# Two weight blocks loaded behind the first keys and queries of an attention and mixture-of-experts kernel

## The chip, the cores and the metric

The kernel runs on one core of one Trainium2 chip. The metric is device time in microseconds (us) of one execution; three timed runs of the kernel before gave 814.26, 817.00 and 824.21 us, median 817.0 us. The core's engines are TensorE (PE, with its weight load PEld), VectorE (DVE), ScalarE (ACT) and GpSimd (POOL); SyncE (SP) issues nearly all of the DMAs. Each engine works through its own list of instructions strictly in order, and semaphores join the lists.

## The reference

Three layers follow one another; all is float32, and the weights of the second layer arrive as 64-bit floats.

```python
# 1. attention, 2 x 8 heads, 576 rows, head size 64; only the 32 largest scores of a row count
scores = scale * np.matmul(q, k.transpose(0, 1, 3, 2))
kth = np.partition(scores, -32, axis=-1)[..., -32:-31]
scores = np.where(scores >= kth, scores, -1e9)
attn = softmax(scores)                      # spelled out in the reference
x = np.matmul(attn, v)                      # to 1152 tokens x 512
# 2. dense layer: w_in 512 x 2048, w_out 2048 x 512
h = x @ w_in
g = np.maximum(h, 0.0) + alpha * np.minimum(h, 0.0)
x = g @ w_out
# 3. eight experts, 512 -> 1024 -> 512; each token goes to its two best, by noisy gate logits
h = np.maximum(x[mask] @ w1[e], 0.0)
out[mask] += top2_w[mask, k, None] * (h @ w2[e])
```

## The kernel before, in words

**Order of the work.** The kernel is straight-line code whose order comes from a small planner (class Order, line 150 on). Every piece of work is a Python generator that asks for engines, buffers and results; the planner keeps a rank for each and a modelled time, and gives a free engine to the waiting step of the lowest rank. A step of the form (engine, cost, extra, shift) may carry a shift that is added to its rank for that one step. What the planner decides is frozen as the order of instructions on each engine; on the chip an engine waits where the planner's time was too early.

**Attention.** For each batch and each pair of heads the keys are loaded (kb, load_pair), split in a rounded part and its remainder (prep: ACT copy L450, then a subtraction L461 on POOL or, for the first pair, on DVE) and transposed on PE (L423) into kp. Queries (qb) go the same way (L510, L514, L423, then a copy to qt on ACT, L428, or on DVE, L430). A unit is two heads of one tile of 128 queries. PE forms the scores (L582), ACT copies them (L598), DVE folds the two halves (L612, L616, L619) and finds the 32nd largest by rounds of MAX8 and MATCH_REPLACE8 (L633, L636); ACT and POOL build the masked exponentials (L670, L672, L676); PE transposes them (L693) and multiplies by the values (vb, L717).

**Dense layer.** Its 16 blocks of w_in and w_out give 32 conversions, `convert(i)`, i even for w_in and odd for w_out. One loads 128 x 512 words of 64 bits (raw, 512 KB, L820 or L822), makes 32-bit floats of them with three DVE instructions (L835, L837, L840), tests their size on ACT (magnitude, L890 and L894), splits them in a rounded part (ACT, L874) and a remainder (POOL, L876) and stores both (L856). The blocks are multiplied (L948, L992) for five groups of token tiles; the first group uses them as they are converted.

**Fillers.** Where the planner's model has PE idle early on, it inserts matmuls of ones (L1728) whose result nobody reads.

**Experts.** After the last group come gate, routing, gathers and the expert layers (L1507, L1542).

The lines around the change: XD is a new constant beside the others (line 73 of the changed kernel, so that all later lines stand one number higher there); the load step of convert; the rank with which the main part adds convert. There, t is the time planned for the first group, CB is 20.0 and CT is 7.5, so conversion 0 has rank 1.5 before and conversion 1 has rank 9.0. The keys of the second pair have rank 0.3, the values 0.8 and up, the split of the second pair of keys 5.0, the first unit's top-k 8.0.

Of the kernel before, what the change touches and what calls it, by code (L numbers as in the profile page):

```python
# [53 lines left out]
NR, NF, NR2, CB, KE, CT = 3, 2, 2, 20.0, 0, 7.5  # L54
# [15 lines left out]
DG, DX, DS = 1.0, 2.0, 0.5  # L70
YC, YL = 0.65, 4.0
NK, FB1 = 4, 12.0
OL, PL = 8.0, 10.0
BEGIN = (("DMA", 1.7), ("ACT", 1.9), ("DVE", 1.5), ("POOL", 1.0))


def split(v):
    return v.bitcast(F32)
# [31 lines left out]
PE, ACT, DVE, POOL, DMA = "PE", "ACT", "DVE", "POOL", "DMA"  # L110
# [25 lines left out]
class Order:  # L136
# [99 lines left out]
    def take(self, *names, room=1):  # L236
        def got():
            for w in names:
                if self.held.get(w, 0) < room:
                    self.held[w] = self.held.get(w, 0) + 1  # L240
                    return w
        return "until", got

    def give(self, what):
        self.held[what] -= 1
        self.given[what] = self.now
        self.at(self.now, 1, self.scan)

    def mark(self, *what):
        self.made.add(what)  # L250
        self.at(self.now, 1, self.scan)

    def need(self, *what):
        return "until", lambda: what in self.made
# [9 lines left out]
def block_kernel(ctx: ExitStack, tc: tile.TileContext, q, k, v, w_in, w_out, alpha,  # L264
# [19 lines left out]
    order = Order()  # L284
# [525 lines left out]
    def convert(i):  # L810
        fb, half = divmod(i, 2)
        w = w_out if half else w_in
        u = 2 if WIDE else 1
        yield take("raw", room=NR)
        yield DMA, 0.75 * u, 2.0
        raw = a1.tile([128, 512 * u], I32 if WIDE else F32, name="raw", bufs=NR)
        if WIDE:
            w = w.bitcast(I32)
        if half:
            nc.sync.dma_start(raw, w[fb * 128:(fb + 1) * 128, :])  # L820
        else:
            nc.sync.dma_start(raw.rearrange("p (c f) -> p c f", c=4),  # L822
                              w[:, fb * 128 * u:(fb + 1) * 128 * u].rearrange("(c p) f -> p c f", p=128))
        if WIDE:
            if i:
                yield need("wf", i - 1)
            yield take("wf", room=NF)
            mark("wf", i)
            f = a2.tile([128, 512], I32, name="wf", bufs=NF)
            rv = raw.rearrange("p (n t) -> p n t", t=2)  # L830
            hi, lo = rv[:, :, 1], rv[:, :, 0]
            yield take("words")
            yield DVE, 0.6
            t = ps.tile([128, 512], F32, name="y1").bitcast(I32)
            V.tensor_scalar(t, hi, 3, 0x3FFFFFFF, op0=OP.logical_shift_left, op1=OP.bitwise_and)  # L835
            yield DVE, 0.65
            V.scalar_tensor_tensor(t, hi, -0x40000000, t, op0=OP.bitwise_and, op1=OP.bitwise_or)  # L837
            order.add(order.rank + 20, magnitude(i, hi.bitcast(F32)))
            yield DVE, 0.65
            V.scalar_tensor_tensor(f, lo, 29, t, op0=OP.logical_shift_right, op1=OP.bitwise_or)  # L840
            f = f.bitcast(F32)
            yield FIN
            give("words")
        else:
            f = raw
        wt, tag = yield from halves(fb, half, f, POOL, fb >= KE)
        yield FIN
        order.add(order.rank, keep(wsc[fb, half], split(wt).rearrange("p a n -> p (a n)"), "hl", fb, half))
        give("wf" if WIDE else "raw")
        if fb < KE:  # L850
            yield need("hl", fb, half)
            give(tag)

    def keep(dst, src, *key):
        yield DMA, 1.5, KL
        nc.sync.dma_start(dst, src)  # L856
        yield FIN
        mark(*key)
# [5 lines left out]
    def halves(fb, half, f, eng, use=True):  # L864

        if use and fb:
            yield need("wt0", half, 0, fb - 1)
        tag = yield take(*places[half])
        wt = a2.tile([128, 2, 512], R32, name=tag)
        if use:  # L870
            WT[0, fb, half] = wt, tag
            mark("wt0", half, 0, fb)
        yield ACT, 0.52
        nc.scalar.activation(wt[:, 0], f, AF.Copy)  # L874
        yield (POOL, pool(512)) if eng == POOL else (DVE, dve(512))
        (nc.gpsimd if eng == POOL else V).tensor_sub(wt[:, 1], f, split(wt)[:, 0])  # L876
        if use:
            order.add(order.rank, marked("wt", 0, fb, half), order.now + (pool(512) if eng == POOL else dve(512)) + HOP)
        return wt, tag
# [6 lines left out]
    def magnitude(i, hi):  # L886
        yield take("mag")
        yield ACT, act(512)
        mag = a1.tile([128, 512], BF, name="mag")
        nc.scalar.activation(mag, hi, AF.Square)  # L890
        yield FIN
        give("raw")
        yield ACT, act(512, 2)
        nc.scalar.activation(mag, mag, AF.Relu, bias=bcon[:, 3:4], scale=-2.0 ** 28, accum_out=least[:, i:i + 1])  # L894
        yield FIN
        give("mag")
        mark("mag", i)
# [6 lines left out]
    def load_kept(g, i, half):  # L904
        fb = block_of(g, i)
        yield need("hl", fb, half)
        if g or i:
            yield need("wt0", half, *((g, 0 if g and i == KB else i - 1) if i else (g - 1, 15)))
        tag = yield take(*places[half])
        yield DMA, 1.5, 2.0  # L910
        wt = a2.tile([128, 2, 512], R32, name=tag)
        nc.sync.dma_start(split(wt).rearrange("p a n -> p (a n)"), wsc[fb, half])
        WT[g, i, half] = wt, tag
        mark("wt0", half, g, i)
        yield FIN
        mark("wt", g, i, half)
# [868 lines left out]
    t = 0.0  # L1785
    for g, ts in enumerate(GROUPS):
        t = max(t, ready[g])
        late = g == len(GROUPS) - 1
        work = len(ts) * 1.3
        step = work if late else max(work, (ready[g + 1] - t) / 16)  # L1790
        for fb in range(16):
            for half in range(2):
                if (g and fb >= KB) or (not g and fb < KE):
                    order.add(t - 10.0 + 4 * half + MO, load_kept(g, fb, half), max(t - 40.0, 0.0))
                if not g:
                    order.add(min(t - CB + 4 * half, 1.5 + CT * (2 * fb + half)), convert(2 * fb + half))
            order.add(t + MO, moe1_block(g, fb))
            t += step
        ranks["gate", g] = t - (GB if late else 0.0)
        order.add(ranks["gate", g], gate(g))  # L1800
# [258 lines left out]
```

## Time and profile before

| what | value |
|---|---|
| timed runs | 814.26, 817.00, 824.21 us; median 817.0 us |
| profiled execution, its own time | 811.02 us |
| its span, first to last instruction | 809.3 us |
| busy: PE, PEld, DVE, ACT, POOL | 752.3, 685.8, 606.2, 506.4, 358.1 us |
| mean granted TensorE clock | 0.972 of 2.4 GHz |
| moved by DMA | 156.62 MB, mean 194 GB/s |

The profile shows one execution. Busy time is a sum over stages with different limits, so a stage has to be read by itself: a table of busy time in stretches tells which engine has no idle time left there, the timeline of one engine shows the gap before each instruction and what ended it, and the order of issue of the loads is in the rows of SP. The profiled execution was 6.0 us shorter than the median of the timed runs.

### The profile page before, as it was taken

The numbers are of one execution on the slowest core, as the hardware profiler recorded it, in microseconds if no ns is written. First come the engines' busy times: TensorE is split into PE (matmuls) and PEld (weight loads), VectorE is DVE, ScalarE is ACT, GpSimd is POOL, SyncE is SP. The second block draws the span as 40 slices with busy tenths as digits, with TensorE's granted clock in tenths as the row PEclk, the third lists the DMA queues.
The fourth block names the chain that finished last, engine by engine and source line by source line (L and its number), as shares of the span: only waits on it lengthen the run. The fifth ranks groups of instructions, "written<-read, shape, count | busy, mean of one in ns | idle before, by whom it ended". The sixth has DMA issues, their size and how long they took to land. (4 is left out here: it accounts for less than half of the span.)

```text
span 809.3 us, 15510 instructions
## 1 busy us (share of the span) xinstructions
PE 752.3 (93%) x5238; PEld 685.8 (85%) x5238; DVE 606.2 (75%) x1713; ACT 506.4 (63%) x1081; POOL 358.1 (44%) x402
## 2 busy tenths in 40 slices
PE   8999878769999999999999999989899998999994
PEld 6888767668898998899988988878799997999983
DVE  6999999998988888898889545167567756667632
ACT  6878897897588778576747642264545544455331
POOL 3655665665575555454445434302422424131313
PEclk9999998688999999999999999999999999999998
DMA  9444689851446402465247559988889988986631
GB/s 277 138 157 122 196 284 321 291 177 64 134 148 193 156 28 94 150 229 181 104 132 234 183 181 304 347 218 198 239 247 242 264 212 245 254 255 180 203 103 59
DMA packets 99851, 156.62 MB, mean 194 GB/s; under 512 B 15902, under 2 KB 65582, under 8 KB 99764
## 3 DMA queue, kind: packets, MB, share of 16 engines
q1 hardware_dynamic: 94260, 145.04, 58.6%
q0 software_dynamic: 5504, 10.51, 4.5%
q8 instruction: 43, 0.70, 0.4%
q14 instruction: 44, 0.36, 0.1%
HBM read 126.76 MB, written 29.34 MB: 193 GB/s over the span
## 5 line engine op out<-in xcount | busy, mean ns | idle before, releaser
L672 POOL TENSOR_TENSOR low<-s_sb,low 128x576 f32<-128x576 f32 x72 | 102.5, 1425 | 81.6 <-ACT low L670 81.6
L948 PE MATMUL h_ps<-xh,wi 128*128 128x256 f32 (+1 forms) x576 | 123.9, 294 | 3.3 <-DVE gf L966 2.6
L948 PEld LDWEIGHTS h_ps<-xh,wi 128*128 128x128 f32 x576 | 98.0, 196 | 8.4 <-DVE gf L966 4.4
L633 DVE MAX8 tk<-rest 128x8 f32<-128x296 f32 x216 | 97.7, 459 | 1.1
L992 PE MATMUL y<-wo,gh 128*128 128x512 f32 x288 | 96.7, 417 | 1.3 <-ACT gh L976 1.3
L979 POOL TENSOR_TENSOR gl<-gf,gh 128x256 fp32r<-128x256 f32 (+1 forms) x80 | 56.6, 709 | 67.3 <-ACT gh L976 65.5
L948 PE MATMUL h_ps<-xl,wi 128*128 128x256 f32 (+1 forms) x288 | 83.4, 289 | 0.0
L717 PE MATMUL x_ps<-vb,pT 128*128 128x64 f32 (+1 forms) x640 | 79.7, 270 | 3.7 <-ACT pT L696 3.3
L717 PEld LDWEIGHTS x_ps<-vb,pT 128*128 128x128 f32 (+1 forms) x640 | 74.7, 187 | 9.9 <-ACT pT L696 6.6
L1298 ACT ACTIVATE w2o<-raw 128x512 fp32r<-128x512 f32 (+1 forms) x60 | 40.4, 711 | 57.2 <-PE x_ps L1542 31.6
L1301 DVE TENSOR_TENSOR w2o<-raw,w2o 128x512 fp32r<-128x512 f32 (+1 forms) x60 | 45.5, 790 | 35.6 <-ACT w2o L1298 28.8
L1507 PE MATMUL s_ps<-xeh,w2i 128*128 128x336 f32 (+1 forms) x256 | 64.9, 315 | 3.8 <-DVE hl L1523 3.8
L1542 PE MATMUL y<-hh,w2o 128*128 128x336 f32 (+1 forms) x288 | 66.9, 316 | 0.0
L636 DVE MATCH_REPLACE8 rest<-tk,rest 128x296 f32<-128x296 f32 x144 | 64.8, 451 | 0.0
L1507 PE MATMUL h_ps<-xeh,w2i 128*128 128x336 f32 (+1 forms) x256 | 63.3, 313 | 0.4 <-DVE hl L1523 0.4
L676 ACT ACTIVATE low<-low,bias 128x576 f32<-128x576 f32 x72 | 55.7, 774 | 12.3 <-POOL low L672 12.2
L582 PE MATMUL s_ps<-kp,qt 128*128 128x288 f32 (+2 forms) x336 | 60.9, 310 | 1.9 <-DVE rest L616 1.9
L598 ACT ACTIVATE s_sb<-s_ps 128x576 f32<-128x576 f32 x72 | 46.9, 651 | 22.9 <-PE s_ps L582 22.3
L992 PE MATMUL y<-wo,gl 128*128 128x512 f32 x144 | 58.6, 407 | 2.1 <-POOL gl L979 1.4
L670 ACT ACTIVATE low<-s_sb,bias 128x576 f32<-128x576 f32 x72 | 55.6, 774 | 7.7 <-POOL bias L641 7.6
L1323 POOL DMA_INDIRECT xg<-x,meta x21 | 25.7, 1225 | 72.2 <-DMA xl<-xg 28.9
L948 PEld LDWEIGHTS h_ps<-xl,wi 128*128 128x128 f32 x288 | 56.5, 196 | 0.7 <-issue 0.3
(315 smaller groups left out, 2069.4 us busy)
## 6 DMA issues: line engine op xcount, KB each, us to landing
raw<-in_moe_w_dram SPq DMA_DIRECT2D x60, 512.0 KB
wi<-wsc SPq DMA_DIRECT2D x48, 512.0 KB
wo<-wsc SPq DMA_DIRECT2D x48, 512.0 KB
raw<-in_moe_w_in_dram SPq DMA_DIRECT2D x16, 512.0 KB
raw<-in_moe_w_out_dram SPq DMA_DIRECT2D x16, 512.0 KB
wsc<-wi SPq DMA_DIRECT2D x16, 512.0 KB
wsc<-wo SPq DMA_DIRECT2D x16, 512.0 KB
raw<-in_moe_w_dram SPq DMA_DIRECT2D x48, 128.0 KB
```

The costliest lines, as they stand in the source:

```text
L582: nc.tensor.matmul(s_ps[:, j, o:o + c1 - c0], l, r[:, c0:c1], start=(i == 0), stop=(i == len(steps) - 1 and (c < 4 or c1 != S)))
L633: V.max(tk[:, 8 * i:8 * i + 8], src)
L636: V.match_replace(rest, tk[:, 8 * i:8 * i + 8], src, -3.0e38)
L670: nc.scalar.activation(low, SC[ht], AF.Relu, bias=bi[:, 1:2], scale=-BIG)
L672: nc.gpsimd.tensor_sub(low, SC[ht], low)
L676: nc.scalar.activation(low, low, AF.Exp, bias=bi[:, 0:1], scale=SCALE, accum_out=SM[part][:, col:col + 1])
L717: nc.tensor.matmul(o, pT[:, i, cs], vb[b, hh // 2][:, s, i * 64:(i + 1) * 64], start=(first and hh == h and i == 0), stop=False)
L948: nc.tensor.matmul(h_ps, l[:, d, :], r[:, d, 0:gn], start=(n == 0), stop=(n == 11))
L979: nc.gpsimd.tensor_sub(gl, gf, split(gh))
L992: nc.tensor.matmul(Y1[g][t], l[:, t * 128:(t + 1) * 128], r, start=(i == 0 and n == 0), stop=(i == 15 and n == 2))
L1507: nc.tensor.matmul(h_ps, l[:, d, s * 128:(s + 1) * 128], r[:, d, :], start=(n == 0), stop=(n == 11))
L1542: nc.tensor.matmul(YP[e][b][:, 0:c], l[:, s, bs], r[:, 0:c], start=(fb == 0 and n == 0), stop=(fb == 7 and n == 2))
```

## The change

Conversions 0 and 1 (the first blocks of w_in and w_out) both get rank 3.0, where they had 1.5 and 9.0. Their load step carries a shift of -2.65, so the loads stand at rank 0.35, right behind the keys of the second pair (0.3). Nothing is computed in another way and no work is added or taken out, but for what the planner decides differently in consequence.

```diff
+XD = -2.65
...
         yield take("raw", room=NR)
-        yield DMA, 0.75 * u, 2.0
+        yield DMA, 0.75 * u, 2.0, XD if i < 2 else 0.0
...
                 if not g:
-                    order.add(min(t - CB + 4 * half, 1.5 + CT * (2 * fb + half)), convert(2 * fb + half))
+                    order.add(3.0 if 2 * fb + half < 2 else min(t - CB + 4 * half, 1.5 + CT * (2 * fb + half)), convert(2 * fb + half))
```

The queue of SP, from the second pair of keys on, in the kernel before (kb keys, vb values, vtail and qtail the last 64 rows of values and queries, raw the 64-bit weights):

```order
L374 DMA kb<-in_k_dram 128x2x256
L374 DMA vb<-in_v_dram 128x2x256
L396 DMA vtail<-in_v_dram 64x4x64 x2
L383 DMA qtail<-in_q_dram 64x8x64
L374 DMA vb<-in_v_dram 128x2x256 x2
L374 DMA kb<-in_k_dram 128x2x256
L374 DMA vb<-in_v_dram 128x2x256
L822 DMA raw<-in_moe_w_in_dram 128x4x256
L820 DMA raw<-in_moe_w_out_dram 128x1024
L374 DMA kb<-in_k_dram 128x2x256
```

The same place in the changed kernel:

```order
L375 DMA kb<-in_k_dram 128x2x256
L823 DMA raw<-in_moe_w_in_dram 128x4x256
L821 DMA raw<-in_moe_w_out_dram 128x1024
L375 DMA vb<-in_v_dram 128x2x256
L375 DMA kb<-in_k_dram 128x2x256
L397 DMA vtail<-in_v_dram 64x4x64 x2
L384 DMA qtail<-in_q_dram 64x8x64
L375 DMA vb<-in_v_dram 128x2x256 x3
L375 DMA kb<-in_k_dram 128x2x256
```

The two weight blocks have moved ahead of all values and of the third pair of keys, which itself has moved ahead of three of the values.

The list of DVE from the second remainder of queries on, before (s_sb and s_ps are the scores, tk and rest the folded ones, wf the converted weights):

```order
L514 TENSOR_TENSOR low<-qb,low 128x512
L430 CAST qt<-y_211 128x512
L612 TENSOR_TENSOR tk<-s_sb,s_ps 128x288
L616 TENSOR_TENSOR rest<-s_sb,s_ps 128x288
L619 MAX tk<-rest 128x8
L633 MAX tk<-tk 128x8
L636 MATCH_REPLACE rest<-tk 128x296
L633 MAX tk<-rest 128x8
L612 TENSOR_TENSOR tk<-s_sb,s_ps 128x288
L835 TENSOR_SCALAR y_287<-raw 128x512
L616 TENSOR_TENSOR rest<-s_sb,s_ps 128x288
L837 SCALAR_TENSOR_TENSOR y_287<-raw,y_287 128x512
```

The same place in the changed kernel:

```order
L515 TENSOR_TENSOR low<-qb,low 128x512
L836 TENSOR_SCALAR y_206<-raw 128x512
L838 SCALAR_TENSOR_TENSOR y_206<-raw,y_206 128x512
L613 TENSOR_TENSOR tk<-s_sb,s_ps 128x288
L841 SCALAR_TENSOR_TENSOR wf<-raw,y_206 128x512
L617 TENSOR_TENSOR rest<-s_sb,s_ps 128x288
L836 TENSOR_SCALAR y_260<-raw 128x512
L620 MAX tk<-rest 128x8
L838 SCALAR_TENSOR_TENSOR y_260<-raw,y_260 128x512
L634 MAX tk<-tk 128x8
L841 SCALAR_TENSOR_TENSOR wf<-raw,y_260 128x512
L613 TENSOR_TENSOR tk<-s_sb,s_ps 128x288
```

Conversion 0 now stands ahead of the first fold and conversion 1 is woven into the first one and the second; the copy of the last quarter of queries (L430) has left DVE's list, and ACT's list has one more copy to qt in its place. From the third conversion on, the conversions stand at the same count of folds as before (within one, for one of them). On POOL the remainders of both conversions (L876) now stand ahead of the splits of the third and the fourth pair of keys (L461). PE's list has 407 fillers in place of 424; behind its last score matmul there are 59 in place of 47, 22 in place of 15 in one run of them.

## Rows read from the trace of the kernel before

**Rows 1.** The page, part 2: busy tenths in 40 slices of 20.2 us.
```profile
PE   8999878769999999999999999989899998999994
DVE  6999999998988888898889545167567756667632
```

**Rows 2.** Stretches of 20 us: length, busy (count) by engine, clock, DMA share, GB/s.
```profile
100.00:120.00 20.00, 13.96 (x95) 12.05 (x96) 19.27 (x49) 19.94 (x48) 14.54 (x16) 0.97 0.85 279
...
140.00:160.00 20.00, 14.61 (x74) 13.03 (x73) 18.99 (x50) 16.61 (x39) 12.27 (x14) 0.66 0.84 285
160.00:180.00 20.00, 13.29 (x90) 11.52 (x88) 19.19 (x52) 17.81 (x43) 14.61 (x16) 0.91 0.60 208
180.00:200.00 20.00, 19.65 (x130) 18.47 (x131) 17.01 (x57) 14.66 (x34) 11.18 (x14) 0.83 0.11 41
...
220.00:240.00 20.00, 20.00 (x151) 18.59 (x150) 17.46 (x59) 17.41 (x43) 14.68 (x19) 1.00 0.52 172
```

**Rows 3.** Stretches of 10 us, same columns.
```profile
10.00:20.00 10.00, 8.83 (x71) 6.97 (x69) 8.75 (x22) 7.64 (x19) 4.66 (x6) 1.00 0.97 315
20.00:30.00 10.00, 9.23 (x78) 7.75 (x77) 9.84 (x29) 10.00 (x23) 7.44 (x9) 1.00 0.48 173
```

**Rows 4.** Timeline of DVE: start, length, instruction, idle before and what ended it.
```profile
8.65 0.68 DVE L514 TENSOR_TENSOR low<-qb,low 128x512 fp32r<-128x512 f32 x1
...
10.16 0.69 DVE L430 CAST qt<-y 128x512 fp32r<-128x512 f32 x1 [0.83 <-PE y L423]
...
10.77 0.44 DVE L612 TENSOR_TENSOR tk<-s_sb,s_ps 128x288 f32<-128x288 f32 x1
...
14.18 0.46 DVE L612 TENSOR_TENSOR tk<-s_sb,s_ps 128x288 f32<-128x288 f32 x1 [0.54 <-ACT s_sb L598]
...
15.05 0.69 DVE L835 TENSOR_SCALAR y<-raw 128x512 int32<-128x512 int32 x1 [0.42 <-DMA raw<-in_moe_w_in_dram]
...
16.99 0.67 DVE L840 SCALAR_TENSOR_TENSOR wf<-raw,y 128x512 int32<-128x512 int32 x1
```

**Rows 5.** Timeline of SP's queue, same columns: issues of loads.
```profile
3.22 0.51 SPq L374 DMA_DIRECT2D kb<-in_k_dram  x1
3.77 0.47 SPq L374 DMA_DIRECT2D vb<-in_v_dram  x1
...
7.68 0.37 SPq L374 DMA_DIRECT2D kb<-in_k_dram  x1
...
9.46 0.37 SPq L822 DMA_DIRECT2D raw<-in_moe_w_in_dram  x1
```

**Rows 6.** DMA view, 0 to 20 us: rate in 40 slices of 0.5 us.
```profile
GB/s 0 0 0 43 106 342 266 360 378 306 209 317 356 346 354 354 309 250 225 198 287 348 350 346 348 350 348 348 402 401 389 346 359 348 348 217 0 123 246 401
```

**Rows 7.** Timeline of ACT, POOL and PE, columns of rows 4: first users of the loads.
```profile
3.60 0.63 ACT L450 ACTIVATE prep<-kb 128x512 fp32r<-128x512 f32 x1 [1.57 <-DMA kb<-in_k_dram]
...
5.74 0.63 ACT L510 ACTIVATE low<-qb 128x512 fp32r<-128x512 f32 x1 [1.51 <-DMA qb<-in_q_dram]
...
12.81 0.63 ACT L450 ACTIVATE prep<-kb 128x512 fp32r<-128x512 f32 x1 [0.52 <-DMA kb<-in_k_dram]
...
13.52 1.27 POOL L461 TENSOR_TENSOR prep<-kb,prep 128x512 fp32r<-128x512 f32 x1 [2.42 <-ACT prep L450]
...
16.67 0.79 PE L582 MATMUL s_ps<-kp,qt 128*128 128x288 f32 x4
```

**Rows 8.** Lines L428, L835 (shortest/median/longest ns); DVE's waits, 20 to 200 us.
```profile
L428 ACT ACTIVATE qt<-pt x16: 575/600/624, 9.2 to 360.4; 128x512 fp32r<-128x512 f32 x16
...
L835 DVE TENSOR_SCALAR y<-raw x32: 666/678/695, 15.1 to 175.3; 128x512 int32<-128x512 int32 x32
...
DVE tk L612 <- ACT s_sb L598: 4.5, 6, 2.2
```

**Rows 9.** Timeline of PE behind the last attention unit, columns of rows 4.
```profile
497.76 1.81 PE L1728 MATMUL x_ps<-ones 128*128 128x256 bf16 x15
...
500.38 0.50 PE L992 MATMUL y<-wo,gl 128*128 128x512 f32 x1 [0.34 <-issue]
```

## The prediction

> **What bounds the kernel now.** I first read where each engine has no time left. The slices of the page [rows 1] show the two regimes: VectorE (DVE) is at nine tenths from the second slice to about 180 us, and from there to the end of the dense layer TensorE (PE) is. The table of stretches [rows 2] makes this sharper: from 100 to 180 us DVE is busy for 19.0 to 19.3 of 20 us while PE stands idle for 5 to 7 us in the three stretches shown, because it waits for attention units; from 180 us PE is busy for 19.65 and later for 20.00 of 20 us. So up to 180 us the kernel goes as fast as DVE's list, and after that PE works off what is left. A microsecond by which DVE's list runs earlier before 180 us lets PE begin its full stretch a microsecond earlier, and should come out at the end; work merely moved within full DVE time gains nothing.
>
> The change touches the first 20 us. There DVE is not yet full: 8.75 of 10 us from 10 to 20, against 9.84 from 20 to 30 [rows 3]. The timeline tells why [rows 4]: behind the second remainder of queries, which ends at 8.65 + 0.68 = 9.33 us, DVE stands 0.83 us for a transposition (before the copy L430), 0.54 us for the second pair of scores and 0.42 us for the first weight block: 1.79 us in all. After that DVE meets no gap in that view up to 20 us. The conversions are 32 times three instructions of some 0.68 us [rows 8], a stock of work that needs nothing but its weights; idle time early on can be filled with it, if the weights are there.
>
> **The change, part by part.**
>
> *When the first block arrives.* The queue of SP and the bytes decide it. Before, the block was issued at 9.46 us [rows 5] and DVE, which waited for it, got it at 15.05 [rows 4], 5.6 us later, because the loads ahead of it had to move first. I test whether loads arrive in the order of issue by adding up bytes along the rate view [rows 6], sizes from the tile shapes (4 bytes per number, 0.262 MB for a pair of keys or values, 0.524 MB for half the queries or a weight block, 0.131 MB for the rows at the end). First keys: 0.262 MB have passed at 3.1 us, used at 3.60. First queries: 0.786 MB at 4.65, used at 5.74. Third pair of keys: 3.015 MB at 11.97, used at 12.81, where ACT waited for it [rows 7]. First weight block: 3.80 MB at 14.20, used at 15.05. Both late ones came 0.85 us behind their bytes, so order of issue explains them. In the changed queue the first weight block is the sixth load: 0.262 + 0.524 + 0.131 + 0.524 + 0.262 + 0.524 = 2.23 MB, which pass at 9.37; plus 0.85 gives an estimate of **10.2 us**. It takes the place of the first values, issued at 3.77 [rows 5], so the issue itself is early enough. The second block follows at 2.75 MB, 11.2 + 0.85 = 12.1 us.
>
> *What DVE gains.* Its list now has the conversion right behind 9.33. It waits to 10.2, 0.87 us, about what it waited before for the transposition. From there it has a conversion whenever a fold is not ready: three instructions of conversion 0 with the first fold between them, then conversion 1, whose block (12.1) is needed only about 13 us. So the later gaps of 0.54 and 0.42 are filled, and idle time falls from 1.79 to 0.87: **-0.92 us**. The copy L430, 0.69 us on DVE [rows 4], goes to ACT: **-0.69**. Sum **-1.6 us**.
>
> *What it costs elsewhere.* ACT takes one copy more, 0.60 us [rows 8], and the early part of two conversions; from 10 to 20 us it has 10.00 - 7.64 = 2.4 us free, which hides them, but from 20 to 30 it has none [rows 3]. Without that cover the copy would cost 0.6. The third pair of keys comes later by bytes: 3.28 MB, 12.73 + 0.85 = 13.6 in place of 12.81; and on POOL a remainder of 1.27 us (as the split of the same size [rows 7]) now precedes its split. That split began at 13.52. Conversion 0 ends on DVE about 12.7 (10.2, two instructions, the first fold, one more), ACT rounds it by 13.4, POOL is through with its remainder at 14.7, and then splits the keys to 16.0. PE has the third score matmul, which began at 16.67 [rows 7], behind their transpositions in its list; it goes to some 17.3, ends about 18.1, and its copy on ACT is through by some 18.8, and DVE comes to the third fold only about 19.5 (start to start its listed instructions take 0.37 to 0.6 us from 10.2 on). That is hidden, with 0.7 us to spare. The values come up to 3 us later; the first multiplication by them needs a finished top-k and its exponentials, so nothing waits. The fourth pair of keys has the same bytes ahead of it and does not move. Unmoved also is the rest of the conversions, which stand at the same folds as before.
>
> *SP.* Before, the issues at 7.68 and 9.46 stood behind earlier waits [rows 5]; the moved blocks, sixth and seventh in the queue, follow the second keys at 3.22 directly. No engine waits for SP in the rows of this stretch.
>
> *Fillers.* Behind the last score matmul there are 12 more, 7 of them in the run that had 15. That run took 1.81 us, 0.12 us each [rows 9]; if PE has other work there, 12 of them cost up to 1.4 us. I take zero, since after the run PE still stood 0.34 us before the third matmul of the block [rows 9]: what it was to multiply was not there. The bound of 1.4 goes into the range.
>
> The bounds of the sum: at best all 1.79 and the 0.69 are gained, -2.5 us. Against the profiled execution's own 811.0 us the forecast of -1.6 gives 809.4; that execution was 6.0 us under the median of the timed runs, so on their footing it is 817.0 - 1.6 = **815.4 us**.
>
> **The rivals.**
>
> *ACT takes it back (0.22).* ACT is full from 20 to 30 us, and again from 100 to 120 with 19.94 of 20 [rows 2, 3]. If it sets the pace there, a DVE that is 1.6 us ahead waits for the copies of the scores; it waits for them 4.5 us in six waits between 20 and 200 us as it is [rows 8]. Then the lead is spent and the time is that of before, **817.0**. Against it: 4.5 of 180 us is little, and DVE's 19.0 to 19.3 of 20 show it as the tighter one.
>
> *The blocks come late, and the first fold stands behind them: slower (0.13).* DVE works strictly in order, so fold one, ready at 10.77, cannot pass conversion 0. If the loads in flight share the engines and do not go in order, the first block lands with the second, the first values and the third keys, at 3.28 MB, 13.6 us. DVE then waits 13.6 - 9.33 = 4.3 us, against a stock of 1.79 + 0.69 = 2.5: **+1.8 us, 818.8**. It decides from a landing at 9.33 + 2.5 = 11.8 us on. For it speaks that the changed queue puts half a megabyte more behind it at once; against it the two loads that came in order within 0.85 us. The Trainium skill, "DMA: Bandwidth & Descriptors", section "Queues, rings and completion order", says that completion is not first-in, first-out per issuing engine, since a later load may finish its writes before an earlier one. By that rule the stall could come, and the sum would be the 818.8 of this rival; the trace, where the two loads that can be checked came in order of issue, does not show it here.
>
> *PE's clock falls elsewhere (0.15).* From 140 to 200 us the granted clock is 0.66, 0.91 and 0.83 between its two levels of 1.2 and 2.4 GHz, after stretches in which PE stood idle [rows 2]. From 180 on PE is the bound, and 20 us at 0.83 cost it 20 x 0.17 = 3.4 us. The order of PE's list shifts all along, so this stretch may come out at full clock, **815.4 - 3.4 = 812.0**, or be followed by another one like it, **818.8**; I take both alike.
>
> *The change does nothing it says (0.05).* The rank may move the loads but DVE's lead may be lost in its own few waits before 180 us, without ACT: 817 again. The forecast itself has 0.45.
>
> **How the numbers follow.** The time is that of the forecast, 815.4 us. The range is set by the runs more than by the cases: the cases lie between 812.0 and 818.8, the bound of the gain under the profiled execution's own time gives 811.0 - 2.5 = 808.5, and at the top I add some 2 us for the scatter of a median, whose runs before lay between 814.3 and 824.2. That gives 808 to 821 us. About 2% (16 us) is what a measurement of this kernel can tell from no change. No case comes near it: 0.02 for faster by more (800.7 or less), 0.02 for slower by more (833.3 or more), left for something unforeseen, and 0.96 within.
>
> **What would show it right or wrong.** In the profile of the changed kernel, the first conversion on DVE should begin at 10.0 to 10.5 us, with a wait for the weight load before it; a start behind 11.8 would be the slower rival. DVE should then show no gap to 20 us and be busy for over 9.5 of the 10 us from 10 to 20. The third pair of keys should reach ACT at about 13.6, the third fold should begin near 19.5 without a wait. The lead should still stand at 180 us: conversion 31, whose first instruction began at 175.3 us before [rows 8], should begin some 1.6 us earlier, in spite of ACT's full stretches; if it begins at 175, ACT took the lead back. Lastly the first instant at which PE is full should come earlier by the same. A change of more than 5 us in either direction would be wrong by more than this sum can hold, and would have to lie in PE's clock or in the run of fillers behind 480 us.

## The result, and the profile after

The changed kernel takes 822.48 us (median of 21 runs, 815.27 to 832.93), the kernel before in the same job 815.52 (median of 21): 7.0 us more, a ratio of medians of 1.0085. The ratio taken over the faster runs of each kernel, as all ratios below are, is **1.0104, with a 95% interval of 1.0064 to 1.0144**, some 8.5 us. So the kernel is slower by 7.0 to 8.5 us, which is within the 2% called the same. The forecast was 815.4 us, 1.6 less than before, with a range of 808 to 821. The profiled execution took 824.87 us, its span 823.1 at a mean clock of 0.962; before it was 811.02, 809.3 and 0.972. The two profiles lie 13.8 us apart, so they show more than the typical loss.

I read the profile in the order of time. The timeline of DVE after, with the columns of [rows 4], shows the front of the list as it was forecast:

```profile
8.88 0.69 DVE L431 CAST qt<-h_ps 128x512 fp32r<-128x512 f32 x1 [1.26 <-PE h_ps L424]
...
9.68 0.68 DVE L515 TENSOR_TENSOR low<-qb,low 128x512 fp32r<-128x512 f32 x1
10.28 0.69 DVE L836 TENSOR_SCALAR y<-raw 128x512 int32<-128x512 int32 x1
...
11.88 0.46 DVE L613 TENSOR_TENSOR tk<-s_sb,s_ps 128x288 f32<-128x288 f32 x1 [0.18 <-ACT s_sb L599]
...
13.21 0.69 DVE L836 TENSOR_SCALAR y<-raw 128x512 int32<-128x512 int32 x1
...
20.14 0.45 DVE L613 TENSOR_TENSOR tk<-s_sb,s_ps 128x288 f32<-128x288 f32 x1 [0.29 <-ACT s_sb L599]
```

The first conversion starts at 10.28 and waits for nothing, so its block was there. The gaps of [rows 4] behind the second remainder of queries (L515 now) are gone but for 0.18 us, and the next is 0.29 at the third fold. A new one of 1.26 us stands ahead of the remainder, which ends at 10.36 in place of 9.33 in this execution; other executions of this front differ there, as the account of the prediction shows. SP issued both blocks right behind the second keys (3.23), where [rows 5] has the values:

```profile
3.77 0.47 SPq L823 DMA_DIRECT2D raw<-in_moe_w_in_dram  x1
4.29 0.50 SPq L821 DMA_DIRECT2D raw<-in_moe_w_out_dram  x1
```

The stretches of after, columns of [rows 2] (the two of 10 us answer to [rows 3]):

```profile
10.00:20.00 10.00, 9.22 (x75) 7.46 (x74) 9.63 (x25) 9.29 (x21) 6.17 (x6) 1.00 1.11 342
20.00:30.00 10.00, 9.24 (x77) 7.62 (x75) 9.39 (x27) 9.34 (x21) 6.23 (x8) 1.00 0.35 122
100.00:120.00 20.00, 14.40 (x78) 12.83 (x78) 19.17 (x52) 19.84 (x47) 13.57 (x16) 0.74 0.84 277
140.00:160.00 20.00, 13.41 (x76) 11.92 (x75) 18.50 (x49) 18.05 (x42) 13.36 (x14) 0.76 0.87 304
160.00:180.00 20.00, 17.30 (x94) 15.93 (x95) 19.70 (x55) 17.70 (x43) 12.91 (x15) 0.67 0.52 166
180.00:200.00 20.00, 19.06 (x135) 17.30 (x135) 16.64 (x58) 14.81 (x33) 9.94 (x14) 0.90 0.18 66
```

DVE has 9.63 of 10 us where it had 8.75. PE's granted clock lies elsewhere than before (0.74 against 0.97 from 100 to 120 us, 0.67 against 0.91 from 160 to 180). Conversion 31 starts 2.8 us earlier than in [rows 8]:

```profile
L836 DVE TENSOR_SCALAR y<-raw x32: 666/680/705, 10.3 to 172.5; 128x512 int32<-128x512 int32 x32
```

So nothing is lost in the part that was changed. Where it is lost, a few instants of both timelines tell (us; the last score matmul L582, the last x of the attention L782, the last matmuls by w_in and w_out, L948 and L992, the scatter of the routing slots, the end of the span; lines of before):

| | last scores | last x | last w_in | last w_out | slots | span |
|---|---|---|---|---|---|---|
| before | 446.4 | 468.1 | 522.3 | 529.5 | 554.6 | 809.3 |
| after | 444.9 | 469.1 | 526.9 | 538.8 | 565.9 | 823.1 |

After is 1.5 us ahead at the last scores and 9.3 behind at the last matmul by w_out: 10.8 us in between, where the diff touches nothing. Another 2.0 us are lost up to the slots and 2.5 in the expert layers behind them. The waits of PE in that part (engine, tile, line, releaser: us in total, times, longest), first before, 444 to 532 us:

```profile
PE y L992 <- ACT gh L976: 1.2, 1, 1.2
PE y L992 <- POOL gl L979: 0.8, 1, 0.8
PE h_ps L948 <- ACT gf L960: 0.5, 1, 0.5
PE y L992 <- issue: 0.3, 1, 0.3
```

and after, 443 to 541 us:

```profile
PE h_ps L1729 <- ACT gf L961: 2.9, 1, 2.9
PE y L993 <- DMA wo<-wsc: 1.5, 1, 1.5
PE y L993 <- ACT gh L977: 1.5, 2, 0.9
PE y L993 <- issue: 1.0, 1, 1.0
PE y L993 <- POOL gl L980: 0.8, 1, 0.8
PE x_ps L718 <- ACT pT L697: 0.7, 1, 0.7
PE s_ps L949 <- DMA wi<-wsc: 0.7, 1, 0.7
```

2.8 us of waits have become over 9, and dense weights and a copy of ACT are among them. ACT's timelines say why. Before, ACT rounded the third block of expert weights (L1298) early, with a wait of 1.09 us:

```profile
490.63 1.06 ACT L1298 ACTIVATE w2i<-raw 128x1024 fp32r<-128x1024 f32 x1 [1.09 <-DMA raw<-in_moe_w_dram]
```

After:

```profile
518.68 0.42 ACT L977 ACTIVATE gh<-gf 128x256 fp32r<-128x256 f32 x1 [0.94 <-PE y L993]
528.63 1.06 ACT L1299 ACTIVATE w2i<-raw 128x1024 fp32r<-128x1024 f32 x1 [9.53 <-DMA raw<-in_moe_w_dram]
529.59 0.36 ACT L961 ACTIVATE gf<-h_ps 128x256 f32<-128x256 f32 x1
```

L1299 is the same rounding. It now waits 9.53 us for its load, and the last copies of the dense layer (gf, L961) stand behind it in ACT's list. The first of them starts at 529.59, although PE had its products by w_in ready at about 524.8: 4.8 us late. (The Trainium skill, "Perfetto Trace Analysis", section "Tensor Engine Instruction (MATMUL, LD_WEIGHTS)", calls ACT's execution queue strict first-in, first-out; these 4.8 us are what that costs here.) The load is the third of the expert weights. SP's timeline after:

```profile
514.61 3.08 SPq L1283 DMA_DIRECT2D raw<-in_moe_w_dram  x4
517.79 1.46 SPq L913 DMA_DIRECT2D wo<-wsc  x2
```

and before:

```profile
481.67 1.85 SPq L1282 DMA_DIRECT2D raw<-in_moe_w_dram  x4
```

Before, it went out 33 us earlier; now it goes out ahead of the last two blocks of w_out, which come late in their turn. The fillers of [rows 9] are now 22, and PE stands 1.00 us behind them:

```profile
498.19 2.58 PE L1729 MATMUL x_ps<-ones 128*128 128x256 bf16 x22
...
502.24 0.50 PE L993 MATMUL y<-wo,gl 128*128 128x512 f32 x1 [1.00 <-issue]
```

Of the 10.8 us, idle time of PE is 6.5 (9.5 against 3.0, summed over stretches). The other 4.3 are busy time: 12 more fillers at 0.12 us, about 1.2 us of a lower clock behind 527 us, and 1.1 us for eight matmuls by the values (48 in place of 40) that before stood ahead of the last scores; some 0.6 us are not accounted for.

### The profile page after: what moved, and what is told of

Same layout as the page of the kernel before. It is cut to its first block, busy times and chain, and to the rows that moved or that the text cites. A ratio compares the mean times of both kernels' runs of the same rounds, so it can differ in the third digit from the quotient of the medians.

```text
span 823.1 us, 15442 instructions
## 1 busy us (share of the span) xinstructions
PE 756.5 (92%) x5221; PEld 688.8 (84%) x5221; DVE 605.8 (74%) x1712; ACT 510.0 (62%) x1082; POOL 354.2 (43%) x402
## 5 line engine op out<-in xcount | busy, mean ns | idle before, releaser
L1299 ACT ACTIVATE w2o<-raw 128x512 fp32r<-128x512 f32 (+1 forms) x60 | 40.4, 711 | 58.5 <-PE x_ps L1543 33.0
L1302 DVE TENSOR_TENSOR w2i<-raw,w2i 128x1024 fp32r<-128x1024 f32 x36 | 43.9, 1220 | 23.8 <-ACT w2i L1299 21.6
L993 PEld LDWEIGHTS y<-wo,gh 128*128 128x128 f32 x288 | 50.0, 195 | 9.7 <-issue 2.0
```

The costliest lines, as they stand in the source:

```text
L993: nc.tensor.matmul(Y1[g][t], l[:, t * 128:(t + 1) * 128], r, start=(i == 0 and n == 0), stop=(i == 15 and n == 2))
L1302: V.tensor_sub(lo, x, split(hi))
```

## The experiments

**Theories.** T1: the planner, whose modelled times the change has shifted, writes another order behind the attention, and that order is the loss; its most visible piece is the third expert load. T2: the loss is the run of fillers behind 480 us. T3: the moved work costs the time itself, through PE's clock between 100 and 220 us.

The planner makes a tool of itself here: adding to the *planned* cost of one conversion step, which no instruction carries, changes the order from that step on. So each front can be joined to either order behind it.

**The changed front with the order of before behind it.** To the changed kernel:

```diff
-            yield DVE, 0.6
+            yield DVE, 0.6 + (2.0 if i == 28 else 0.0)
```

> The changed kernel, with 2 us more of planned time for the first step of conversion 28: the changed kernel's order for the first 100 issues of SP and 406 rows of DVE (to about 160 us, first conversion at 10.3 us), then the kernel before's for the last 508 issues of SP, 1531 rows of DVE and 764 of ACT. It is the mirror of the run with the old front and the new rest. T1 (the front is as good as forecast, the loss lies in the order behind it): ratio 0.994 to 1.000, conversion 31 near 173 us, the last output-weight matmul near 527 us, so the forecast of 1.6 us gained holds for this kernel. Rival T3 (the front gives its lead back through PE's clock between 100 and 200 us whatever follows): ratio 1.001 to 1.006.

Measured: **0.9995 [0.9958, 1.0032]**. Conversions from 10.5 to 172.1 us, last scores 444.5, last w_out 528.4, 83.9 us apart as before. The loss is gone with the front left in. In its profile DVE runs 1.9 us ahead of before on the same instructions from 425 to 510 us, and 0.2 behind by 536. The forecast gain of 1.6 us (0.998) lies within the interval, as does none.

**The front of before with the changed order behind it.** To the kernel before, the same line with 1.5 at i == 28:

> The kernel before, with 1.5 us more of planned time for the first step of conversion 28. The order is the kernel before's for the first 109 issues of SP and 407 rows of DVE (to about 160 us, first conversion on DVE at 15.1 us), and the changed kernel's for the last 501 issues of SP, 1531 rows of DVE and 763 of ACT. T1: the loss appears without the changed front, ratio 1.007 to 1.013, ACT waits near 9 us for the third load of expert weights. T3: nothing is lost, ratio 0.997 to 1.003.

Measured: **1.0116 [1.0078, 1.0153]**. The whole loss without any of the change. Last scores to last w_out take 95.5 us, and ACT's timeline has the wait:

```profile
533.41 1.06 ACT L1298 ACTIVATE w2i<-raw 128x1024 fp32r<-128x1024 f32 x1 [10.13 <-DMA raw<-in_moe_w_dram]
```

Compared instruction by instruction, these two kernels go over from the one order to the other between 159 and 190 us. They settle it between T1 and T3. Two more joints, with 2.0 at i == 20 and at i == 6 in the changed kernel:

> The changed kernel, with 2 us more of planned time (not of real time) for the first step of conversion 20. The order is the changed kernel's for the first 82 issues of SP and 321 rows of DVE (to about 100 us), and the kernel before's for the last 528 issues of SP, 1599 rows of DVE and 825 of ACT, the stretch behind the attention among them. Theory T1 (the order that the planner writes behind the attention costs the time): the loss goes, ratio to the kernel before 0.996 to 1.001, the last output-weight matmul near 529 us and the last ACT row of the second weights without its 9.5 us wait. Rival T3 (the work moved to the first 20 us itself costs it, through the clock that PE is granted behind it): the loss stays, ratio 1.006 to 1.012, with PE's clock under 0.8 in two stretches of 20 us between 100 and 200 us.

> The changed kernel, with 2 us more of planned time for the first step of conversion 6: the changed front for the first 60 issues of SP and 196 rows of DVE, and then the kernel before's order for the last 561 issues of SP and 1821 rows of DVE, so that only the first 60 us or so differ from the kernel before. T1: ratio 0.996 to 1.001. T3: ratio 1.001 to 1.006, with PE's clock under 0.8 in the stretch 100 to 120 us, where the kernel before has 0.97.

Measured: 1.004 [1.0002, 1.0079] and 1.0003 [0.9976, 1.0029]. In the first, DVE is 0.7 us ahead of before on the same instructions at 130 us and 1.9 behind at 159, with PE's clock at 0.81 from 120 to 140, where before had 0.85, and 0.77 against 0.97 from 100 to 120; in the second the clock from 100 to 120 is 0.99. The first lies outside what T1 said (0.996 to 1.001), the second within. As the front stands in both, and in the run of 0.9995, and the intervals overlap, the 0.4% of the first need not be the front's; what it is stays open. If T3 holds anything, it is a few tenths of a per cent.

**The halves of the change.** Loads alone, and rank alone, each on the kernel before:

```diff
-        yield DMA, 0.75 * u, 2.0
+        yield DMA, 0.75 * u, 2.0, (-1.15, -8.65)[i] if i < 2 else 0.0
```

```diff
-                    order.add(min(t - CB + 4 * half, 1.5 + CT * (2 * fb + half)), convert(2 * fb + half))
+                    order.add(3.0 if 2 * fb + half < 2 else min(t - CB + 4 * half, 1.5 + CT * (2 * fb + half)), convert(2 * fb + half))
```

> Half of the change: the first two loads are issued behind the first keys and queries, their conversions keep their old ranks. The planner then writes the changed kernel's order behind the attention (last 385 issues of SP and 729 rows of DVE alike). T1: as slow as the changed kernel, ratio 1.007 to 1.013. T3: with the conversions less early, about half, 1.003 to 1.006.

> The other half: the first two conversions get the changed rank, their loads stay where they were. The planner then writes the kernel before's order behind the attention (last 519 issues of SP and 1599 rows of DVE alike). T1: no loss, ratio 0.997 to 1.002. T3: a loss if the conversions come early, about 1.003 to 1.006.

Measured: **1.0162 [1.0095, 1.0229]** (five runs) and **1.0012 [0.9974, 1.0049]**. The half that draws the changed order behind it loses, the other doesn't. The first loses more than T1 said; its clock from 100 to 200 us is the lowest of all (0.59 from 160 to 180), and its last scores come at 451.8.

**The third load by itself.** Put earlier in the changed kernel:

```diff
-        yield DMA, 1.5, 2.0
+        yield DMA, 1.5, 2.0, -20.0 if e == 0 and not late and 2 * ch + half < 3 else 0.0
```

> The changed kernel, with one expert-weight load (the third, 4 x 128 KB) put back from behind nearly all loads of the last group to their middle; nothing before 470 us differs. Theory T1 (this load, issued 33 us later than before, holds up ACT and with it the last two blocks of the dense layer): ACT's wait of 9.5 us ahead of the first line L1299 there falls under 3 us, the last dense matmul comes 5 to 9 us earlier, ratio to the kernel before 0.995 to 1.001. Rival T2 (13 more filler matmuls and the new order behind the attention cost it) and rival T3 (the lower clock from 100 to 220 us costs it): ratio stays 1.007 to 1.012.

Measured: 1.0045 [1.0008, 1.0082], between what T1 and its rivals said. The load is issued at 494.75; last scores to last w_out 88.3 us in place of 93.9. PE now waits for a block of w_in that comes behind it:

```profile
PE h_ps L949 <- DMA wi<-wsc: 1.8, 1, 1.8
PE y L993 <- POOL gl L980: 1.5, 2, 0.8
PE y L993 <- issue: 1.0, 1, 1.0
```

Was the middle still too late? The same edit with -32.0, which issues the second load at 476.38, ahead of the dense weights, and the third at 480.99, behind only two blocks of them:

> The changed kernel, with the third load of expert weights due 32 us sooner in the plan, so that it is issued near 475 us, behind the second load and ahead of the kept dense weights and of the stores of x2 (in the kernel before it stands behind these, at 481.7 us; in the changed kernel at 514.6). Everything to about 440 us is in the changed kernel's order. T1a (the place of this one load in SP's queue is the whole loss, with transfers at under half of the queues' time between 467 and 480 us to carry it): ratio 0.996 to 1.001, last output-weight matmul within 530 us. T1b (the load is half of it, and the later end of the attention outputs, 2.4 us from the last scores to the last output more than before, with what follows from it, is the other half): ratio 1.002 to 1.007, as when the load was put in the middle.

Measured: 1.0048 [1.0018, 1.0078], 87.2 us. That is T1b: of the 10.8 us the place of the load makes 5.6 to 6.7, about half, at either place. Put late in the kernel before instead:

```diff
+        third = (e, ch, half, late) == (0, 1, 0, False)
+        if third:
+            yield need("h1", 4, 13)
...
-        yield DMA, 1.5, 2.0
+        yield DMA, 1.5, 2.0, -8.0 if third else 0.0
```

> The kernel before, with that third expert-weight load held back until block 13 of the last group, three loads from the group's end; the first 470 us are unchanged. T1: the same stall of ACT appears, 5 to 10 us, and the ratio is 1.005 to 1.012 with no change to the front at all. T2 and T3: 0.999 to 1.002, as fillers and front are those of before.

Measured: 1.0021 [0.9983, 1.0058], where T1 had said 1.005 to 1.012: T1's forecast for this run failed. ACT's wait comes, 5.09 us ahead of the same copies, but from the last scores to the last w_out it takes 82.6 us, no more than before. In the kernel before ACT waits 4.04 us for PE ahead of those copies anyway, so a wait of this size need not cost anything there. It is no clean mirror either: the fourth load goes out in the third one's place, at 478.08 in place of 517.38. From the last scores to the slots it takes 113.7 us in place of 108.2, the wait now behind the dense layer; the profiled execution had won 3.6 us ahead of that with an unchanged order. The times don't tell it from no loss.

**ACT's place for it.** In the changed kernel, the rounding is held behind the last dense outputs:

```diff
+        if (e, ch, half, late) == (0, 1, 0, False):
+            yield need("y1", 4, 15)
```

> The changed kernel, all loads in its own order, but ACT's rounding of that third load stands behind the last copies of the dense layer in ACT's list. T1 in its narrow form (the harm is ACT waiting in order ahead of those copies): the dense layer ends 5 to 8 us earlier, ratio 0.997 to 1.004; the waits of 1.5 and 0.7 us for the last dense weights stay. T1 in its wide form (the load clogs the DMA queue, and the experts start late whatever ACT does): ratio 1.005 to 1.010. T2 and T3: 1.007 to 1.012.

Measured over four runs: 1.0121 [1.0035, 1.0208]. Its profile is 5.0 us shorter from the last scores to the slots (116.0 against 121.0), the times are not; inconclusive. ACT was not out of the way either: the rounding of the fourth block now waits for its load ahead of the last gh, and PE waits 3.3 us for that gh.

```profile
532.13 1.06 ACT L1301 ACTIVATE w2o<-raw 128x1024 fp32r<-128x1024 f32 x1 [5.29 <-DMA raw<-in_moe_w_dram]
```

**The fillers.** In the changed kernel, none are placed once the last top-k is found (they feed no output):

```diff
+        if ("top", nu - 1, 1) in order.made:
+            return None
```

> The changed kernel without the 59 filler matmuls behind the last scores; every other instruction stands where it stood. T2: they cost PE time, 59 x 0.12 = 7 us at most, so the ratio falls to 1.000 to 1.003. T1 and T3: they lie in waits, at most 1 to 2 us are won, ratio 1.006 to 1.012; if they keep the clock up, it may even be slower than the changed kernel.

Measured over four runs: 1.0135 [1.0089, 1.0182]. T2 falls, which had said 1.000 to 1.003. In the profile, last scores to last w_out get 2.9 us shorter, 91.0 (that order by itself spreads from 90.9 to 95.5), but the expert layers (first to last matmul of their first product) take 248.0 us in place of 240.9. The stretches show PE's clock, here without the fillers:

```profile
520.00:540.00 20.00, 13.51 (x59) 10.33 (x58) 6.67 (x7) 8.14 (x13) 2.55 (x3) 0.74 1.09 216
580.00:600.00 20.00, 14.85 (x80) 12.95 (x81) 8.00 (x21) 8.19 (x17) 4.73 (x5) 0.74 0.80 210
```

and in the changed kernel:

```profile
520.00:540.00 20.00, 12.60 (x60) 8.68 (x58) 5.17 (x6) 5.18 (x9) 2.56 (x3) 0.91 1.03 214
580.00:600.00 20.00, 13.72 (x78) 11.09 (x77) 8.37 (x20) 7.29 (x15) 8.85 (x9) 0.83 0.78 208
```

**The version the runs point to.** The changed front, the joint at 28, and the third load due 36 us sooner:

> The version that the runs point to: the changed front, the kernel before's order behind 160 us (2 us more of planned time for the first step of conversion 28), and the third load of expert weights due 36 us sooner, near 473 us, where transfers take half of the queues' time. If the idle queues there are worth something, 0.990 to 0.997; if PE's work sets the end of the dense layer, 0.997 to 1.001.

Measured: 1.0007 [0.998, 1.0034]. The load goes out at 470.04 and wins nothing that can be measured. No version beat the kernel before.

**The runs together.** The stretches behind the last scores, by the order they run in:

| order behind | runs | last scores to last x | to last w_out | to slots |
|---|---|---|---|---|
| of before | before and four others | 21.6 to 21.7 | 83.1 to 83.9 | 108.2 to 110.6 |
| of before, third load early | one | 21.6 | 83.3 | 109.4 |
| of before, third load late | one | 21.7 | 82.6 | 113.7 |
| of the change | after and two others | 24.2 to 24.3 | 90.9 to 95.5 | 116.4 to 121.0 |
| of the change, third load early | two | 24.1 to 24.2 | 87.2 to 88.3 | 113.3 to 114.8 |

In the first row and the fourth, where the load itself was not moved, the two orders overlap in no column. The expert layers, from the first to the last matmul of their first product, do not follow the order: they take 236.1 to 244.4 us with that of before and 235.0 to 242.6 with that of the change, fillers kept.

The other half of the loss has its first 2.5 us ahead of the last x: in the changed kernel 8 more matmuls by the values and 4 more by w_in stand between the last scores and that x, 1.8 us of busy time, and PE waits 0.7 us for a tile of exponentials. What the remaining one or two microseconds hang on was not separated, and no run put this half right by itself.

## Why the prediction was wrong

- *Arrival by order of issue (10.2 us): right.* The first block was there by 10.28, with no wait. Eight more profiles have the changed front; in six of them DVE does wait for the block, and starts on it at 9.86 to 11.23. The Trainium skill, "DMA: Bandwidth & Descriptors", section "Queues, rings and completion order", does not promise that order; here too the trace shows it kept, since with the loads behind it the block would have come at 13.6.
- *DVE's gain of 0.92 us in idle time: right in those six, hidden in this execution.* In the six, the wait for the block, forecast as 0.87 us, is 0.80 to 0.89 and the only gap from the remainder to 20 us. In the run without late fillers, for one:

```profile
10.14 0.69 DVE L836 TENSOR_SCALAR y<-raw 128x512 int32<-128x512 int32 x1 [0.88 <-DMA raw<-in_moe_w_in_dram]
```

In the profile of the changed kernel and in two more, 1.11 to 1.33 us of waiting for PE stand ahead of the remainder instead. PE's transpositions are slower there, here one before and one after:

```profile
6.56 0.60 PE L423 MATMUL x_ps<-ident,low 128*128 128x128 f32 x4
```

```profile
6.92 1.06 PE L424 MATMUL x_ps<-ident,low 128*128 128x128 f32 x4
```

The granted clock from 5 to 10 us is 1.00 in both; what slowed them stays open. The third fold, forecast for 19.5, comes at 20.14 here and at 18.98 to 20.45 in the nine; the third keys reached ACT at 14.61, not 13.6, behind other work in its list.
- *A lead of 1.6 us: about right, early.* On the same instruction at 60 us DVE is 1.6 us ahead of before in the changed kernel and 1.2 to 3.2 in all nine profiles, while two with the old front are 0.1 and 0.2 behind. Conversion 31 is no good witness, though I named it as one: in the run with the third load first, whose order to 440 us is that of the changed kernel, it starts at 176.4.
- *"Should come out at the end": unproved.* With the order of before behind it, the front is worth between -0.4% and +0.3%.
- *The step that failed* is the list of the parts. It treated the effects of the change as over at 20 us, but for a displaced clock and 12 fillers, and so put the order behind the attention at nothing, although the order had changed on every engine to the last group. With that order the stretch from the last scores to the last w_out takes 90.9 to 95.5 us, with the order of before 83.1 to 83.9, with either front; joined to the front of before it makes the whole loss (1.0116), and without it the loss is gone (0.9995). I looked for what the change moves near where it was made, and did not read SP's and ACT's lists behind the attention, where a load stood 33 us later than before and its user ahead of the last dense copies. Those lists were there to read. The late load makes about half of what was lost there, 5.6 to 6.7 of 10.8 us; of the rest, 2.5 us are the later last x, and the remainder is open.
- *"Would have to lie in PE's clock or in the run of fillers":* wrong. About half of it lay in the lists of SP and ACT, and of the other half 2.5 us in the order of PE's list. The 12 more fillers take some 1.4 us of PE's time in the profile, but leaving out all late ones won nothing.
- *ACT takes it back, and late blocks:* not seen. *PE's clock elsewhere:* seen, but with either front (last section).

## What to carry to other kernels

Where a planner freezes the order, a change of rank is a change of the whole program. Compare the lists of every engine up to the end, and look first at loads that have changed sides with other loads and at their users on in-order engines. To cost the edit and the reshuffle apart, disturb a planned time so that the planner writes the old order behind the new front, and the new order behind the old front.

## What the runs showed of the hardware

**The same order runs at different clocks.** The changed kernel and the run with the third load first have one order to 440 us. In the second DVE comes 1.0 us earlier at 104 us and 3.9 us later at 158, and PE's clock between 120 and 140 us is 0.99 in the one and 0.83 in the other. Changed kernel:

```profile
120.00:140.00 20.00, 16.64 (x127) 14.77 (x127) 19.96 (x55) 16.19 (x39) 12.26 (x14) 0.99 1.01 319
```

Third load first:

```profile
120.00:140.00 20.00, 17.14 (x109) 15.37 (x110) 17.58 (x46) 15.08 (x36) 10.30 (x13) 0.83 0.88 291
```

PE is short of work there, 17 of 20 us, and yet DVE is set back (19.96 to 17.58). From 80 to 160 us it waits 4.5 us in place of 1.7 for gf, which ACT copies from PE's products, and 1.8 in place of 0.7 for weight blocks; the first fits the low clock, but no run set the clock by itself. Likewise the kernel before and the one with its third load late, alike to 440 us, lie 3.1 us apart at 195. A single profile of this kernel can't show a lead of 2 us behind 120 us. From 200 to 440 us, where PE is busy for 18.0 to 20.0 of 20 us in both kernels, two executions of the same list keep their distance to 0.6 us in five pairs and to 1.4 in a sixth.

**Leaving out the late fillers won nothing.** Without them one execution won 2.9 us ahead of the last w_out and lost 7.1 in the expert layers, whose 248.0 us are the longest of all profiles; the other thirteen have 235.0 to 244.4. Its clock is 0.74 from 580 to 600 us, where the changed kernel has 0.83. Whether the fillers hold the clock up there is not shown: the ratios of the two kernels, 1.0104 and 1.0135, overlap in their intervals.
